# Window attention, forward and backward: GpSimd's gradient loads held until the gradient transpose ahead of them on SyncE has landed

## The chip, the cores and the metric

The kernel runs on one core of a Trainium2 chip. The metric is the device time of one execution in microseconds (us). A ratio is the mean time of one kernel's fast runs over the mean time of the other's fast runs of the same rounds on the same chip, with a 95% interval, so it is not quite the ratio of the medians that are quoted beside it. A run is called slow when it is over 1.5% above the fastest of the same kernel.

Words used throughout: a *transpose* is a DMA that SyncE issues and that turns a tile while it moves it; its *issue* is the time that SyncE spends on it, its *flight* the time from the start of the issue to landing. A *load* and a *store* are plain DMAs.

## The reference, cut to what matters

```python
xw  = windows of 8x8 tokens of x (1, 256, 256, 384)         # 1024 windows of 64 tokens
q, k, v = split(xw @ wqkv)
p   = softmax(q @ k.T * 384**-0.5)
out = windows_back((p @ v) @ wo)
out_0          = out
out_1, 2, 3    = gradients of x, wqkv, wo for a given grad_out
```

Everything is bf16. The kernel uses products of the weights that are formed once, so a window needs its x, its gradient and both of them transposed.

## The kernel before

The 1024 windows are handled eight at a time: 128 "quads" of four pairs. Three quads are in work at once: in step i, quad i-1 (c) is finished, quad i (b) gets its scores and softmax, quad i+1 (a) is projected, and inputs are loaded for a quad further on.

```python
    def load(st):                       # inputs of a quad
        xq = grp.tile(..., bufs=10);  dq = qp.tile(..., bufs=6)
        for t in range(QUAD):
            nc.sync.dma_start(out=xq[:, t, :], in_=windows(x, st, 2 * t))           # SyncE
            nc.gpsimd.dma_start(out=dq[:, t, :], in_=windows(grad_out, st, 2 * t))  # GpSimd

    def load_turn(st):                  # SyncE: dT <- dq, then xT <- xq (12 blocks of 128x128 each)
    ...
    def to_tokens(st):                  # SyncE: tok <- yz, 24 blocks
    def turn(st):                       # SyncE: PS <- ps, 4 blocks
    ...
    def attend(st, pair):
        ...                             # matmuls; ScalarE copies the results to o and d tiles
        for dst, sb, outer in stores:   # six stores a call, 96 or 48 KB each
            nc.gpsimd.dma_start(...)
    ...
    def step(c, b, a, ahead):
        B(scores);  B(soft, 0..4) between B(uv, ...)
        A(project, 0, ...)              # reads dT
        B(soft, 5);  B(turn)
        if ahead is not None:
            load(ahead)
        C_(attend, (0, 1))              # first group of six stores
        A(project, 1, ...)              # reads xT
        A(to_tokens)
        C_(attend, (2, 3))              # second group of six stores
```

In the traces SyncE and GpSimd work their instructions off in program order. Per step SyncE's order is dT, xT, PS, four loads of xq, tok; GpSimd's is four loads of dq, six stores, six stores.

Of the kernel before, what the change touches and what calls it, by code (L numbers as in the profile page):

```python
# [22 lines left out]
def kernel(  # L23
# [21 lines left out]
    nc = tc.nc  # L45
# [61 lines left out]
    def windows(ap, st, first, count=2):  # L107
        row, col = st["at"]
        return ap[0, row + WIN * first:row + WIN * (first + count), col:col + WIN, :]
# [1 line left out]
    LO, HI = slice(0, WT), slice(WT, P)  # L111
    OTHER = {0: HI, WT: LO}

    def load(st):
        st["xq"] = xq = grp.tile([P, QUAD, C], BF16, tag="xq", name="xq", bufs=2 * GQ + 4)
        st["dq"] = dq = qp.tile([P, QUAD, C], BF16, tag="dq", name="dq", bufs=6)
        for t in range(QUAD):
            nc.sync.dma_start(out=xq[:, t, :], in_=windows(x, st, 2 * t))
            nc.gpsimd.dma_start(out=dq[:, t, :], in_=windows(grad_out, st, 2 * t))  # L119
# [59 lines left out]
    def over_k(ap, n=P):  # L179
        return ap.unsqueeze(2).broadcast_to([n, QUAD, WT])  # L180

    def soft(st, step):
        sd = st["sd"]
        if step == 0:
# [122 lines left out]
    def filler(n):  # L307
        while n and fill:
            try:
                next(fill[0])  # L310
                n -= 1
            except StopIteration:
                fill.pop(0)

    def step(c, b, a, ahead):


        def on(st):
            return (lambda f, *r: f(st, *r)) if st is not None else (lambda f, *r: None)
        C_, B, A = on(c), on(b), on(a)  # L320
        B(scores)
        B(soft, 0)
        B(uv, 0, 0)
        B(uv, 0, 1)
        B(soft, 1)
        B(uv, 1, 0)
        B(uv, 1, 1)
        B(soft, 2)
        B(soft, 3)
        B(uv, 2, 0)  # L330
        B(uv, 2, 1)
        for t in range(QUAD):
            A(grad_turn, t)
        B(uv, 3, 0)
        B(uv, 3, 1)
        B(soft, 4)
        for mo in range(CK):
            A(project, 0, mo)
        B(soft, 5)
        B(turn)  # L340
        if ahead is not None:
            load(ahead)
        filler(1)
        C_(attend, (0, 1))
        split[0] = True
        for mo in range(CK):
            A(project, 1, mo)
        A(to_tokens)
        filler(1)
        split[0] = ALL  # L350
        C_(attend, (2, 3))
# [4 lines left out]
    sts = [{"at": q, "i": i} for i, q in enumerate(quads)]  # L356
    n = len(sts)
    AHEAD = 3
    with tc.manual_schedule(engines=MANUAL):
        for i in range(min(AHEAD, n)):  # L360
            load(sts[i])
            if i < AHEAD - 1:
                load_turn(sts[i])
        held = []
        get = lambda i: sts[i] if 0 <= i < n else None
        for i in range(-1, n + 1):
            if AHEAD - 1 <= i + AHEAD - 1 < n:
                load_turn(sts[i + AHEAD - 1])
            step(get(i - 1), get(i), get(i + 1), get(i + AHEAD) if i >= 0 else None)
            if i > 0:  # L370
                held.append(sts[i - 1])
                sts[i - 1] = None
            if held and (len(held) == GQ or i == n):
                fill.append(gf_group(held))
                held = []
        split[0] = False
        filler(1 << 30)
# [62 lines left out]
```

## Time and profile before

| | before |
|---|---|
| time, median of 3 runs | 1999.15 us (1994.77 to 2006.96) |
| span of the profiled execution | 1989.7 us |
| TensorE busy | 1961.3 us |
| an undisturbed step | 15.13 us, all matmuls |
| SyncE's queue, period from tok to tok, mean of quads 15 to 117 | 15.17 us |
| of it issuing / gaps | 14.28 / 0.89 us |

The list of DMA issues on the page of the kernel before (count, then the median flight in us):

```profile
dT<-dq SPq DMA_TRANSPOSE x128, 6.6
xT<-xq SPq DMA_TRANSPOSE x128, 6.8
```

The tile view of tok, before: the issue's duration in ns (least, median, longest), then the flight:

```profile
L167 SPq DMA_TRANSPOSE tok<-yz x128: 3903/4722/7185, 26.2 to 1944.2; - x128
...
DMA to landing us min/median/max: 5.8/8.4/12.3
```

tok is the largest of the four transposes, with a median flight of 8.4 us.

### The profile page before, as it was taken

The numbers are of one execution on the slowest core, as the hardware profiler recorded it, in microseconds if no ns is written. First come the engines' busy times: TensorE is split into PE (matmuls) and PEld (weight loads), VectorE is DVE, ScalarE is ACT, GpSimd is POOL, SyncE is SP. The second block draws the span as 40 slices with busy tenths as digits, with TensorE's granted clock in tenths as the row PEclk, the third lists the DMA queues.
The fourth block names the chain that finished last, engine by engine and source line by source line (L and its number), as shares of the span: only waits on it lengthen the run. The fifth ranks groups of instructions, "written<-read, shape, count | busy, mean of one in ns | idle before, by whom it ended". The sixth has DMA issues, their size and how long they took to land.

```text
span 1989.7 us, 52374 instructions
## 1 busy us (share of the span) xinstructions
PE 1961.3 (99%) x19418; PEld 1122.4 (56%) x19418; DVE 1258.1 (63%) x2851; ACT 1453.4 (73%) x3341; POOL 1122.6 (56%) x2054
## 2 busy tenths in 40 slices
PE   7899999999999999999999999999999999999998
PEld 4455555555555555555555555555555555555555
DVE  4666666666666666666666666566666666666665
ACT  5777777777777777777777777677777777777774
POOL 3555555565556555555655555555555556555543
PEclk9999999999999999999999999999999999999999
DMA  9999999999999999999999999999999999999993
GB/s 202 224 207 222 209 213 226 220 215 225 211 216 223 215 213 214 227 220 217 220 213 219 221 217 210 219 218 223 220 216 216 211 224 214 225 214 219 213 206 102
DMA packets 1042272, 425.62 MB, mean 214 GB/s; under 512 B 925792, under 2 KB 1016672, under 8 KB 1042016
## 3 DMA queue, kind: packets, MB, share of 16 engines
q1 hardware_dynamic: 943312, 270.60, 81.5%
q0 software_dynamic: 98304, 151.39, 31.3%
q8 instruction: 152, 2.49, 0.5%
q14 instruction: 104, 0.85, 0.1%
q10 hardware_dynamic: 400, 0.29, 0.0%
HBM read 101.84 MB, written 101.84 MB: 102 GB/s over the span
## 4 chain that ended last, share of the span: by engine, by line
PE 91%; DMA 7%; ACT 1%; DVE 1%; issue 0%; POOL 0%; SPq 0%; ACTq 0%; POOLq 0%
PE pj L147 33%; PE pj L145 12%; PE pg L147 12%; PE pg L145 12%; PE pd L258 6%; PE pu L253 5%; PE sd L147 5%; PE pw L253 4%; DMA dT<-dq 4%; DMA PS<-ps 2%; ACT uq L229 1%; ACT vq L229 0%; DMA dq<-in_grad_out_dram 0%; DMA xT<-xq 0%; PE pd L253 0%
## 5 line engine op out<-in xcount | busy, mean ns | idle before, releaser
L292 POOL DMA_DIRECT2D out_dram<-o x256 | 139.1, 543 | 693.8 <-ACT o L264 686.4
L304 DVE TENSOR_TENSOR GF_acc<-pg,GF_acc 128x384 f32<-128x384 f32 x258 | 143.8, 557 | 522.5 <-PE pg L145 372.3
L264 ACT CAST o<-po 128x384 bf16<-128x384 f32 x512 | 221.4, 487 | 248.1 <-issue 247.7
L147 PEld LDWEIGHTS <-xT 128*128 128x128 bf16 x3072 | 291.8, 98 | 182.2
L147 PE MATMUL pj<-B_sb,xT 128*128 128x384 bf16 x1536 | 333.4, 326 | 0.0
L147 PE MATMUL pj<-AT_sb,xT 128*128 128x384 bf16 x1536 | 333.3, 326 | 0.0
L119 POOL DMA_DIRECT2D dq<-in_grad_out_dram x512 | 274.2, 548 | 72.5 <-DMA out_dram<-o 39.1
L147 PE MATMUL pj<-dT,BT_sb 128*128 128x512 bf16 x1152 | 269.7, 379 | 5.5 <-DMA dT<-dq 5.3
L145 PE MATMUL pj<-xT,A_sb 128*64 128x512 bf16 x2304 | 271.9, 381 | 1.9 <-DMA xT<-xq 1.8
L229 ACT CAST uq<-pj 128x384 bf16<-128x384 f32 x512 | 247.3, 483 | 31.5 <-PE pj L147 28.4
L229 ACT CAST vq<-pj 128x384 bf16<-128x384 f32 x512 | 250.0, 488 | 2.7 <-ACT uq L229 0.3
L264 ACT CAST d<-pd 128x384 bf16<-128x384 f32 x512 | 227.6, 512 | 0.2 <-ACT o L264 0.2
L147 PEld LDWEIGHTS <-xq 128*128 128x128 bf16 x1572 | 153.7, 98 | 114.8 <-issue 0.3
L145 PEld LDWEIGHTS <-xq 128*64 128x64 bf16 x3000 | 167.9, 110 | 88.9
L207 ACT COPY ps<-Pb 64x256 bf16<-64x256 bf16 x256 | 103.2, 403 | 149.7 <-DVE Pb L204 148.2
L163 ACT CAST yz<-pj 128x512 bf16<-128x512 f32 x384 | 208.5, 659 | 3.6 <-PE pj L145 3.5
L161 ACT CAST yz<-pj 128x512 bf16<-128x512 f32 x384 | 206.4, 645 | 0.3 <-PE pj L147 0.2
L145 PEld LDWEIGHTS <-A_sb 128*64 128x64 bf16 x2304 | 132.4, 110 | 100.2 <-DMA xT<-xq 2.3
L147 PEld LDWEIGHTS <-BT_sb 128*128 128x128 bf16 x1152 | 111.4, 98 | 131.4 <-DMA dT<-dq 11.3
L147 PE MATMUL pg<-Uq,xq 128*128 128x384 bf16 x1032 | 181.6, 326 | 0.0
L253 PE MATMUL pu<-xq,PS 64*64 64x384 bf16 x1024 | 174.9, 335 | 6.4 <-DMA PS<-ps 5.9
L258 PE MATMUL pd<-tok,ps 128*64 128x384 bf16 x1024 | 177.7, 344 | 0.0
(68 smaller groups left out, 3366.6 us busy)
## 6 DMA issues: line engine op xcount, KB each, us to landing
xq<-in_x_dram SPq DMA_DIRECT2D x512, 96.0 KB, 4.1
dq<-in_grad_out_dram POOLq DMA_DIRECT2D x512, 96.0 KB, 4.0
out_dram<-o POOLq DMA_DIRECT2D x256, 96.0 KB, 4.3
out_dram<-o POOLq DMA_DIRECT2D x512, 48.0 KB, 4.4
out_dram<-d POOLq DMA_DIRECT2D x256, 96.0 KB, 4.4
out_dram<-d POOLq DMA_DIRECT2D x512, 48.0 KB, 4.4
dT<-dq SPq DMA_TRANSPOSE x128, 6.6
xT<-xq SPq DMA_TRANSPOSE x128, 6.8
```

The source lines that it names most:

```text
L119: nc.gpsimd.dma_start(out=dq[:, t, :], in_=windows(grad_out, st, 2 * t))
L145: nc.tensor.matmul(out[h], lhsT=lhsT[:, h], rhs=rhs, start=start, stop=stop)
L147: nc.tensor.matmul(out, lhsT=lhsT, rhs=rhs, start=start, stop=stop)
L161: ENG[EV["z"][mo]](out=yz[:, mo, :, 0:4:3, :], in_=pj[:])
L163: ENG[EV["y"][mo]](out=yz[:, mo, :, 1:3, :], in_=pj[:])
L207: nc.scalar.copy(out=ps[h, :, w, :], in_=Pb[h, :, :])
L229: cp(out=dst[:, t, :], in_=pj[:])
L253: nc.tensor.matmul(at[o, :], lhsT=turned(st, lhs, t, h), rhs=st[rhs][h, t, :], **{"start": True, "stop": True, **fl})
L258: nc.tensor.matmul(pd[outer if w == 0 else 1 - outer][o, :], lhsT=st["ps"][:, t, w, :], rhs=st["tok"][:, :, t, w, :], **flags)
L264: nc.scalar.copy(out=sb[:], in_=src[outer][:])
L292: nc.gpsimd.dma_start(out=windows(dst, st, 2 * t0 + 1), in_=sb[:])
L304: nc.vector.tensor_tensor(out=GF_acc[:, f, ma, :], in0=pw[:], in1=GF_acc[:, f, ma, :], op=ALU.add)
```

## The change

The gradient loads for a quad are to wait until the dT of the quad ahead has landed, so that they and the stores after them don't share the DMA engines with it. A copy of one element from that dT into the tile to be loaded makes GpSimd wait.

```diff
-    def load(st):
+    def load(st, behind=None):
         ...
+        if behind is not None:
+            nc.gpsimd.tensor_copy(out=dq[0:1, 0, 0:1], in_=behind[0:1, 0, 0, 0:1])
         for t in range(QUAD):
             nc.sync.dma_start(out=xq[:, t, :], in_=windows(x, st, 2 * t))
             nc.gpsimd.dma_start(out=dq[:, t, :], in_=windows(grad_out, st, 2 * t))
@@ step
         if ahead is not None:
-            load(ahead)
+            load(ahead, sts[ahead["i"] - 1]["dT"])
```

## The prediction

> **What bounds the kernel now.** I read the page first (busy time, DMA rows, issues), then the waits of TensorE's matmuls and weight loads, then the timelines of GpSimd and of SyncE's queue over two steps in the middle, and last the tile view of dT.
>
> ```profile
> PE 1961.3 (99%) x19418; PEld 1122.4 (56%) x19418; DVE 1258.1 (63%) x2851; ACT 1453.4 (73%) x3341; POOL 1122.6 (56%) x2054
> ...
> PEld L147 <- DMA dT<-dq: 11.3, 17, 1.5
> PEld L253 <- DMA PS<-ps: 9.0, 12, 3.5
> ...
> PE pu L253 <- DMA PS<-ps: 5.9, 5, 3.2
> PE pj L147 <- DMA dT<-dq: 5.3, 9, 1.1
> PE pj L145 <- DMA xT<-xq: 1.8, 1, 1.8
> ```
>
> TensorE is busy in 99% of the span. The wait rows (us in total, times, longest) say what all transposes together cost it in 128 steps: at the weight loads 11.3 us for dT and 9.0 us for PS. The last three rows are waits of the matmuls; those for PS and dT are the same waits seen a second time and are not added, the one for xT adds 1.8 us. The sum is 22.1 us, 1.1% of 1989.7 us. In the timeline the scores of successive steps begin at 1004.53 and 1019.66, so an undisturbed step takes 15.13 us, all of it back-to-back matmuls; the step from 1246.60 to 1263.0 took 16.4 us because its first matmuls on dT waited. So TensorE bounds nearly every step, and the transposes only a few of them. The chain of waits credits 4% of the span to dT<-dq, but that counts each transpose's whole flight of about 6.6 us, most of which lies beside matmuls.
>
> The second resource at its limit is the pair of SyncE's queue and the DMA engines:
>
> ```profile
> 999.70 2.84 SPq L128 DMA_TRANSPOSE dT<-dq  x1
> 1002.72 2.85 SPq L128 DMA_TRANSPOSE xT<-xq  x1
> 1005.73 1.20 SPq L233 DMA_TRANSPOSE PS<-ps  x1
> 1006.98 2.55 SPq L118 DMA_DIRECT2D xq<-in_x_dram  x4
> 1009.63 5.32 SPq L167 DMA_TRANSPOSE tok<-yz  x1
> 1015.18 1.45 SPq L128 DMA_TRANSPOSE dT<-dq  x1
> ```
>
> Columns are start, duration, engine, line, transfer. From one dT to the next are 15.48 us with gaps of 0.25 us at most: this queue works without a pause, at the pace of TensorE. Its margin is almost nil, which is why lateness of dT lasts for several steps once it appears.
>
> GpSimd's queue over the same time:
>
> ```profile
> 999.85 0.55 POOL L292 DMA_DIRECT2D out_dram<-o  x1 [4.62 <-ACT o L264]
> ...
> 1004.93 0.54 POOL L292 DMA_DIRECT2D out_dram<-o  x1 [1.75 <-ACT o L264]
> ...
> 1008.21 2.14 POOL L119 DMA_DIRECT2D dq<-in_grad_out_dram  x4
> 1014.98 0.55 POOL L292 DMA_DIRECT2D out_dram<-o  x1 [4.62 <-ACT o L264]
> ...
> DMA to landing us min/median/max: 3.9/6.6/9.6
> ```
>
> Six stores at 999.85, right on top of the dT issued at 999.70; six more at 1004.93; the four gradient loads at 1008.21. The last line is the flight of dT. 12 stores and 4 loads of about 0.55 us are 8.8 us of issue in 15.13, so GpSimd has about 6 us to spare.
>
> **What the Trainium skill says.** "DMA: Bandwidth & Descriptors", section "Issuing engines are not separate DMA queues": transfers issued from any engine run on the same 16 DMA engines and interleave. The trace agrees: the same 12-block transpose flies between 3.9 and 9.6 us, though its size never changes. The same page, "Anatomy of one DMA", says that DMA engines do not wait on semaphores; the wait is on the issuing sequencer before dispatch. That matters here: GpSimd's one-element copy holds everything after it in GpSimd's order, stores included. "GPSIMD Engine Reference", section "2.1 Instruction dispatch", warns that consecutive Pool instructions are not a barrier: a later Pool instruction needs the completion semaphore of the earlier one; the built program has exactly such a wait of the first load on the copy.
>
> **The change part by part.**
> Added: one copy of one element on GpSimd for each of 125 held loads. No row of this trace has such a copy; I estimate 0.4 us with its wait and completion, 50 us of GpSimd over the span, all inside its spare 6 us a step. The order of the built instructions shows nothing else added or removed on any engine; 512 loads, 768 stores and 512 transposes stay.
>
> Moved: which dT the copy waits for. The loads at 1008.21 belong to the quad after the one whose dT is issued next, at 1015.18. That dT lands at about 1015.2 + 6.6 = 1021.8. So this is no small nudge: the loads move from 1008.2 to about 1022, by 13.6 us, almost a step. The stores of the following step, ready from 1014.98 on, move behind them: in place of two groups of six at 1015.0 and 1020.1 there is one burst of twelve from about 1024.4 to 1031 or later.
>
> What this gives: the time from about 8 us before a dT to its landing has fewer of GpSimd's packets. dT now shares its flight with six stores; afterwards with the tail of a burst at most. I expect its flight to fall from 6.6 to about 5 or 5.5 us (the minimum is 3.9). xT gains likewise. tok, which overlaps the burst, loses; but tok causes no wait in this trace and is wanted only half a step or more after it lands. Total bytes and packets are unchanged, so the work of the DMA engines is unchanged, and SyncE's queue should keep a period near 15.1 us. Of the 22.1 us of waits the dT share of 11.3 us could go mostly; I credit 5 us, because PS and the lag of the queue itself remain.
>
> What this costs: the slack of the gradient loads. Before, loads issued at 1008.2 landed near 1008.2 + 1.65 + 4.0 = 1013.9 (three further issues of 0.55 us, then the page's median flight of 4.0 us), and their dT came one step later, at about 1030.2: 16 us of slack. Afterwards there is a closed loop: dT lands (6.6), copy (0.4), issues (1.65), last load lands (4.0), next dT. Sum 12.7 us, against a step of 15.13: it closes with 2.4 us to spare. It overruns only where dT and load are both slow (9.6 and a load near 8 or 10 us). I take 10% of the steps overrunning by 1 us, much of it absorbed since dT is issued some 3 us before it is needed: 12 us lost at most, 4 us credited.
>
> Stores: the o and d staging tiles have 8 buffers each, two steps' worth. A delay of about 9 us leaves more than half a step. I count zero.
>
> Sum: -5 + 4 = about -1 us, with fewer dT waits by shorter flight and a few by late loads. Against the median of 1999.15 us that is 1998; I lean slightly to the good side, 1996.
>
> **The rivals.**
> (1) The loop becomes the bound. If the flights in the new arrangement sum to 15.5 us, each step takes 15.5 and the kernel loses 128 x 0.4 = 50 us: about 2045. For it: the median margin is 2.4 us and the maxima exceed it, and SyncE's queue, once held by a late load, also delays xT, PS, xq and tok behind it. Against it: the loads now enter a GpSimd queue that has been empty for microseconds, in place of following six stores, so they should land faster than 4.0 us from issue.
> (2) A real gain. If SyncE's queue gets shorter without the stores under dT and xT, all 22 us of waits could go: about 1977. No more than that is to be had, because the rest of the span is matmuls; a gain over 2% (40 us) would need the matmuls themselves to shorten. This is why I hold it nearly impossible.
> (3) A store burst that stalls ScalarE: output tiles not free in time. It would show as waits of o and d copies on out_dram. Against it: two steps of buffers; it could cost some 20 us if landing took a whole step.
>
> **Range and chances.** From the best case (1977) and a modestly overrunning loop (0.2 us a step, 25 us, about 2022), and from runs of the unchanged kernel that lie between 1994.77 and 2006.96: 1980 to 2022. Faster by over 2%: 2%. Slower by over 2%: 8%, rival 1. Within 2%: 90%.
>
> **What would show it.** Loads of GpSimd begin within 1 us after a dT landing, with the wait of the copy of some 5 us a step; stores come in one burst of twelve; dT's median flight is below 6.6 us, tok's above 8.4; total TensorE waits on transposes stay between 5 and 30 us; undisturbed steps remain 15.13 us. The prediction is wrong if SyncE's queue shows dT waiting for dq in a large share of the steps, or steps of more than 15.3 us on the average.

## More of the kernel before

The experiments were made in six groups; the kernel before was run beside each, and its median there lay between 1993.78 and 2005.56 us.

A transfer is *outstanding* from the start of its issue to its landing.

## The result, and the profile after

| | before | after |
|---|---|---|
| time, median of 4 runs each | 1996.96 us (1990.1 to 2006.96) | 2112.98 us (2107.65 to 2114.43) |
| ratio, 95% interval | 1 | 1.0572 (1.0522 to 1.0622) |
| span, profiled execution | 1989.7 us | 2111.0 us |
| TensorE's idle time (span less busy time) | 28.4 us | 122.1 us |

The changed kernel is slower by 5.7%. Its busy line and its waits for transposes (total us, times, longest):

```profile
PE 1988.9 (94%) x19418; PEld 1119.6 (53%) x19418; DVE 1258.5 (60%) x2851; ACT 1459.8 (69%) x3341; POOL 1143.6 (54%) x2179
```

```profile
PEld L149 <- DMA dT<-dq: 143.2, 100, 4.5
...
PE pj L149 <- DMA dT<-dq: 98.1, 78, 4.1
...
PEld L255 <- DMA PS<-ps: 1.9, 5, 0.8
```

Weight loads now wait for dT in 100 of 128 steps, for 143.2 us in place of 11.3. In the median dT landed 2.2 us before its first matmul began in the kernel before, and 0.05 us before it now. These waits are not all lost, since a weight load starts while the matmul before it runs; the matmuls' own 98.1 us is nearer to the loss. The whole loss of 121.3 us of span is 93.7 us more idle time of TensorE (122.1 - 28.4) and 27.6 us more busy time (1988.9 - 1961.3). Only dT does this: the waits for PS shrank from 9.0 to 1.9 us.

Yet dT itself flies no longer than before. The page's list of issues, after:

```profile
dq<-in_grad_out_dram POOLq DMA_DIRECT2D x512, 96.0 KB, 3.2
...
dT<-dq SPq DMA_TRANSPOSE x128, 6.6
xT<-xq SPq DMA_TRANSPOSE x128, 5.8
```

So dT is not slow; it is issued late. SyncE's timeline over two steps says why (start, duration, line, transfer):

```profile
1025.63 2.50 SPq L130 DMA_TRANSPOSE dT<-dq  x1
1028.30 3.07 SPq L130 DMA_TRANSPOSE xT<-xq  x1
1031.53 1.19 SPq L235 DMA_TRANSPOSE PS<-ps  x1
1032.78 2.51 SPq L120 DMA_DIRECT2D xq<-in_x_dram  x4
1035.39 6.86 SPq L169 DMA_TRANSPOSE tok<-yz  x1
1042.49 1.68 SPq L130 DMA_TRANSPOSE dT<-dq  x1
```

From dT to dT are 16.86 us here. Nothing stands between the entries: SyncE waits for no data here. (The view of SyncE's waits books 582.3 us in front of tok to ScalarE's yz. That is no such wait: tok's issue begins 10.9 us in the median, and never less than 8.2 us, after the last part of yz is written, against 8.2 and 6.3 us in the kernel before.) The entry that grew is tok, 6.86 us against 5.32 in the step that the prediction shows. The tile view of tok, after, confirms it for the whole run:

```profile
L169 SPq DMA_TRANSPOSE tok<-yz x128: 3957/6050/7858, 22.5 to 2065.5; - x128
...
DMA to landing us min/median/max: 5.8/11.3/13.5
```

What goes on beside tok is in GpSimd's timeline over the same step (in brackets the idle time before and what ended it):

```profile
1032.22 0.18 POOL L118 COPY dq<-dT 1x1 bf16<-1x1 bf16 x1 [6.19 <-DMA dT<-dq]
1032.79 2.14 POOL L121 DMA_DIRECT2D dq<-in_grad_out_dram  x4 [0.39 <-POOL dq L118]
1034.88 0.57 POOL L294 DMA_DIRECT2D out_dram<-o  x1
...
1038.20 0.54 POOL L294 DMA_DIRECT2D out_dram<-o  x1
...
1044.90 0.56 POOL L292 DMA_DIRECT2D out_dram<-d  x1
```

The copy waits 6.19 us for dT, as intended; the loads go out at 1032.79; and then the stores that had to stand behind them go out, from 1034.88, in a run. That is exactly where tok (1035.39 to 1042.25) is being issued. I counted, from issue and landing of every store, how many were outstanding on the average while tok was issued: 0.8 before, 5.3 after.

SyncE's queue by kind of issue, worked out from the start and end of every DMA issue of SyncE in the trace (means, quads 15 to 117, us a step, the period from tok to tok):

| | dT | xT | PS | 4 xq | tok | issues | gaps and waits | period |
|---|---|---|---|---|---|---|---|---|
| before | 2.14 | 3.01 | 1.49 | 2.74 | 4.89 | 14.28 | 0.89 | 15.17 |
| after | 2.35 | 2.97 | 1.34 | 2.47 | 6.03 | 15.16 | 1.04 | 16.20 |
| difference | +0.21 | -0.04 | -0.15 | -0.27 | +1.14 | +0.88 | +0.15 | +1.03 |

1.03 us times 128 steps is 132 us, beside 121 us of lost span. The 0.15 us is SyncE's wait for late gradient loads (21.1 us in nine waits in the whole run). The loss is thus a longer period of SyncE's queue, and of that 1.14 us is tok, 0.15 late loads, and the rest nearly cancels.

A smaller part has to do with TensorE's clock. The timeline of TensorE and the view by stretches (us, busy time of PE, PEld, DVE, ACT, POOL with counts, granted clock, DMA share, GB/s), after:

```profile
1015.05 3.53 PE L149 MATMUL pj<-dT,BT_sb 128*128 128x512 bf16 x9 [2.36 <-DMA dT<-dq]
```

```profile
1015.00:1019.00 4.00, 3.95 (x11) 1.52 (x12) 0.50 (x2) 1.88 (x4) 3.58 (x7) 0.57 1.00 227
```

After an idle gap of 2.36 us the granted clock was 0.57 over the next 4 us, and the nine matmuls on dT took 3.53 us; at full clock a step later they took 2.12 us. There were seven such stretches inside the loop, one before. They account for some 12 of the 27.6 us of longer busy time (lost clock summed over the records: 14.7 us after, 3.1 before).

### The profile page after: what moved, and what is told of

Read it like the earlier page. It is cut to its first block, busy times and chain, and to the rows that moved or that the text cites. A ratio compares the mean times of both kernels' runs of the same rounds, so it can differ in the third digit from the quotient of the medians.

```text
span 2111.0 us, 52749 instructions
## 1 busy us (share of the span) xinstructions
PE 1988.9 (94%) x19418; PEld 1119.6 (53%) x19418; DVE 1258.5 (60%) x2851; ACT 1459.8 (69%) x3341; POOL 1143.6 (54%) x2179
## 2 busy tenths in 40 slices
DMA packets 1042274, 425.64 MB, mean 202 GB/s; under 512 B 925792, under 2 KB 1016672, under 8 KB 1042016
## 5 line engine op out<-in xcount | busy, mean ns | idle before, releaser
L149 PE MATMUL pj<-dT,BT_sb 128*128 128x512 bf16 x1152 | 280.1, 390 | 105.6 <-DMA dT<-dq 98.1
L149 PEld LDWEIGHTS <-BT_sb 128*128 128x128 bf16 x1152 | 106.6, 99 | 257.7 <-DMA dT<-dq 143.2
L118 POOL COPY dq<-dT 1x1 bf16<-1x1 bf16 x125 | 26.2, 210 | 394.9 <-DMA dT<-dq 357.0
L294 POOL DMA_DIRECT2D out_dram<-d x256 | 138.6, 542 | 181.8 <-DMA out_dram<-o 66.0
L291 POOL DMA_DIRECT2D out_dram<-d x256 | 144.1, 563 | 126.5 <-ACT d L266 52.7
L292 POOL DMA_DIRECT2D out_dram<-d x256 | 144.1, 563 | 82.2 <-DMA out_dram<-d 68.7
```

What stands on the lines that cost most here:

```text
L149: nc.tensor.matmul(out, lhsT=lhsT, rhs=rhs, start=start, stop=stop)
L291: nc.gpsimd.dma_start(out=windows(dst, st, 2 * t1 + 1, 1), in_=sb[LO, :])
L292: nc.gpsimd.dma_start(out=windows(dst, st, 2 * t0, 1), in_=sb[HI, :])
L294: nc.gpsimd.dma_start(out=windows(dst, st, 2 * t0 + 1), in_=sb[:])
```

## The experiments

Two theories at the start. **Queue**: the held stores come out in a burst while SyncE issues tok; tok's issue gets longer, SyncE's in-order queue falls behind TensorE, and dT is late. **Loop**: dT, copy, loads, next dT form a closed circle that has become the bound. Below, "stores at tok" is the average number of outstanding stores during tok's issue; period, issues and tok are means worked out as above. dT wait is that of the weight loads.

| run | median us | ratio (95%) | period | issues | gaps, waits | tok issue | stores at tok | dT wait |
|---|---|---|---|---|---|---|---|---|
| before | 1996.96 | 1 | 15.17 | 14.28 | 0.89 | 4.89 | 0.8 | 11.3 |
| after | 2112.98 | 1.057 (1.052-1.062) | 16.20 | 15.16 | 1.04 | 6.03 | 5.3 | 143.2 |
| d_older | 1992.16 | 0.999 (0.994-1.004) | 15.17 | 14.27 | 0.90 | 4.80 | 0.7 | 14.6 |
| b_last | 2024.47 | 1.015 (1.011-1.020) | 15.46 | 13.88 | 1.58 | 4.63 | 0.7 | 33.0 |
| c_stores | 2083.57 | 1.044 (1.040-1.048) | 16.01 | 15.10 | 0.90 | 5.72 | 6.0 | 100.6 |
| a_between | 2105.14 | 1.054 (1.048-1.060) | 16.20 | 15.12 | 1.08 | 5.97 | 5.2 | 139.9 |
| e_tok | 2114.74 | 1.058 (1.056-1.060) | 16.15 | 15.25 | 0.90 | 5.72 | 4.6 | 151.7 |
| h_pause | 2001.82 | 1.004 (0.999-1.010) | 15.36 | 14.46 | 0.90 | 4.44 | 1.4 | 44.1 |
| i_later | 2054.73 | 1.030 (1.027-1.033) | 15.76 | 14.86 | 0.89 | 5.12 | 1.2 | 74.2 |
| l_tiny | 2004.32 | 1.005 (1.003-1.007) | 15.25 | 14.35 | 0.90 | 4.62 | 0.6 | 10.8 |
| s_swap | 2041.05 | 1.018 (1.014-1.022) | 15.63 | 14.72 | 0.90 | 5.18 | 4.2 | 43.2 |
| v_burst | 2091.87 | 1.047 (1.043-1.051) | 16.01 | 15.12 | 0.89 | 5.47 | 3.6 | 122.1 |
| w_xq | 2039.35 | 1.022 (1.019-1.025) | 15.62 | 14.27 | 1.35 | 4.51 | 0.4 | 28.3 |
| t_drop (wrong result) | 1977.02 | 0.987 (0.983-0.990) | 15.03 | 12.06 | 2.97 | 4.24 | 2.1 | 1.4 |
| u_drop (wrong result) | 1979.72 | 0.992 (0.990-0.994) | 15.09 | 13.87 | 1.22 | 4.74 | 1.0 | 0 |
| x_after_act | 2021.26 | 1.013 (1.010-1.015) | 15.46 | 11.81 | 3.65 | 4.96 | 2.3 (estimate) | 3.1 |
| y_before_act (3 fast runs) | 2075.13 | 1.040 (1.037-1.044) | 15.88 | 14.30 | 1.58 | 5.85 | 6.3 | 30.4 |
| z_half_act | 1988.36 | 0.996 (0.994-0.999) | 15.14 | 13.79 | 1.35 | 5.21 | 5.2 | 1.1 |

One thing to see before the single runs: in before, c_stores, d_older, e_tok, h_pause, i_later, l_tiny, s_swap and v_burst the gaps are 0.89 or 0.90 us. There SyncE waits for nothing between its issues, and its period is the sum of its issues plus this constant. It's these issues that stretch and shrink. This sum says where the time is, not what made it; for that the runs have to be compared. f_after_xq and g_before_xq, two failed tests, are left out of the table. In x_after_act the trace lacks the landing of 644 of the 1536 stores; they are counted with the median flight of their kind. The profiled execution of h_pause was the slowest of its four, 2016 us, so the last five entries of its row are on the bad side.

### What the copy costs

d_older keeps all 125 copies, but each asks for a dT one quad older, which has long landed.

```diff
-            load(ahead, sts[ahead["i"] - 1]["dT"])
+            load(ahead, sts[ahead["i"] - 2]["dT"])
```

> The copy reads the dT of one quad earlier, which has landed by then: same 125 copies, nothing is held. Both theories: 1990 to 2010. If the copies themselves cost (a third theory, C), above 2030.

1992.16 us, the same as before (the interval is -0.6 to +0.4%). The copies as such are free; all that follows comes from when transfers start.

### Loads late, stores free

b_last puts the copy and the four gradient loads at the end of GpSimd's step, behind both groups of stores, so no store stands behind the copy's wait but those of the next step.

```diff
         C_(attend, (2, 3))
+        if ahead is not None:
+            load_grad(ahead, sts[ahead["i"] - 1]["dT"])   # copy and four dq loads; xq loads stay
```

> The copy and loads stand behind both store groups, so no store is held; the loads are issued at the same place within the step as before the change, for a quad that is one step nearer. Theory A: 1990 to 2015, tok issue near 4.8. Theory B (loads too close to their own dT): slower than 2090, with SyncE's queue waiting for dq in most steps.

1.5% slower, not 5.7%, between the ranges of the two theories. SyncE's issues are even shorter than before (13.88 us), tok's is 4.63 us; the loss comes from SyncE waiting for gradient data, 94.9 us in 44 waits against 21.1 in nine in the changed kernel. Late loads cost something when they come this late, but it is another cost than the one sought.

### Stores late, loads free

c_stores issues the loads unheld and puts the same wait, with a copy into a spare tile, between them and the first group of stores.

```diff
-            load(ahead, sts[ahead["i"] - 1]["dT"])
+            load(ahead)
+            hold = sm.tile([P, 1], BF16, tag="hold", name="hold")
+            nc.gpsimd.tensor_copy(out=hold[0:1, 0:1], in_=sts[ahead["i"] - 1]["dT"][0:1, 0, 0, 0:1])
```

> The copy stands behind the loads and writes a scratch tile: loads are never short of slack, but all twelve stores of a step wait for the dT and go out in one burst. Theory A: as slow as the changed kernel, 2080 to 2130, tok issue about 6. Theory B: 1990 to 2010.

4.4% slower: most of the loss with loads that are in good time (SyncE waited for them 6.3 us in three waits). The circle through the loads is not needed for it. Six stores are outstanding during tok's issue, and that issue is 5.72 us. This points to Queue.

### Only one group of stores held

I took the harm for that of a run of twelve, made because the first group has to wait. a_between therefore puts the copy and loads between the two groups.

```diff
         C_(attend, (0, 1))
+        if ahead is not None:
+            load_grad(ahead, sts[ahead["i"] - 1]["dT"])
         split[0] = True
```

> The copy and the four gradient loads stand between the two store groups of a step; the loads still wait for the same dT and start at the same time as in the changed kernel, only the first six stores go out undelayed. Theory A (the loss comes from the twelve delayed stores that go out in one burst under the tok transpose and stretch its issue on SyncE's queue, 6.05 us against 4.7): most of it comes back, time below 2040, tok issue median below 5.3. Theory B (the closed loop dT, copy, loads, dT sets the period of 16.2): loop unchanged, time 2095 to 2125.

5.4% slower: a miss for me, with a time in the range that Loop (B in the expectation) gave. GpSimd's timeline in this run shows that I had rearranged nothing:

```profile
1000.19 2.13 POOL L127 DMA_DIRECT2D dq<-in_grad_out_dram  x4 [0.39 <-POOL dq L125]
1002.29 0.56 POOL L300 DMA_DIRECT2D out_dram<-o  x1
...
1005.62 0.54 POOL L300 DMA_DIRECT2D out_dram<-o  x1
```

The second group stands behind the loads, and the first group of the next step right behind the second: again loads and a long run of stores, at the same place on the clock. An order that repeats every step has no beginning; only the place of the wait in the circle counts.

### The burst moved away from tok, by tok's own landing

e_tok holds the stores of the kernel before until that step's tok has landed.

```diff
             load(ahead)
+        if b is not None and c is not None:
+            hold = sm.tile([P, 1], BF16, tag="hold", name="hold")
+            nc.gpsimd.tensor_copy(out=hold[0:1, 0:1], in_=b["tok"][0:1, 0, 0, 0, 0:1])
```

> As c_stores, but the copy waits for the landing of the tok transpose and not of a dT: again all twelve stores of a step are held and go out in one burst, only now after tok. Theory A' (what costs is stores lying under the tok transpose, wherever they were ready): tok issue below 4.9 us, period back at 15.13, time 1985 to 2015. Theory D (any hold of stores or any burst of twelve costs, by delay or by crowding): 2050 to 2130, as c_stores.

5.8% slower, another miss. tok lands so late that twelve stores after it are still being worked off when the next tok is issued: 4.6 stores at tok, tok's issue 5.72 us. The stores missed one tok's flight and met the next one's issue. The run doesn't speak against Queue, but the edit didn't do what I meant.

### The loads of x moved to GpSimd: two failed tests

To give SyncE slack I let GpSimd issue the four loads of x, in the changed kernel (f_after_xq) and in the kernel before (g_before_xq).

```diff
-            nc.sync.dma_start(out=xq[:, t, :], in_=windows(x, st, 2 * t))
+            nc.gpsimd.dma_start(out=xq[:, t, :], in_=windows(x, st, 2 * t))
```

> The changed kernel with its four xq loads a step issued by GpSimd ahead of the copy, so that SyncE's queue has 2.6 us less to issue a step. Theory A (SyncE's queue, stretched by tok to 16.2 us a step, is the new bound): its period falls under 15.13 and the time comes back to 1985 to 2030. Theory B or any theory in which the chain through dT and the loads is the bound: 2090 or more.

> The kernel before with the same move of the xq loads; control for f_after_xq and a candidate that beats it. Theory A: SyncE's queue gets slack, the waits on transposes (22 us) shrink: 1975 to 1995. If GpSimd with 20 transfers a step is too full: above 2000.

2305.87 us (1.154, 1.148 to 1.160) and 2271.1 us (1.136, 1.133 to 1.139). With 20 transfers a step GpSimd delivers gradients too late: SyncE waited for them 547.3 and 422.8 us in total. The tests replaced one overload by another and tell nothing of the change. They do tell something of tok: its issue took 6.22 and 6.46 us with only 1.9 and 2.1 stores beside it, so stores are not all that counts. The right engine for this test was ScalarE; see the last group.

### The pause at other places

h_pause lets the loads wait for the softmax of the same step (the tile ps), about the moment at which GpSimd stood idle anyway; i_later leaves the loads free and holds the first group of stores until the last projection of the step is written.

```diff
-            nc.gpsimd.tensor_copy(out=dq[0:1, 0, 0:1], in_=behind[0:1, 0, 0, 0:1])
+            nc.gpsimd.tensor_copy(out=dq[0:1, 0, 0:1], in_=behind[0:1, 0, 1, 0:1])
@@ step
-            load(ahead, sts[ahead["i"] - 1]["dT"])
+            load(ahead, b["ps"])
```

> No store is held and no load waits for a dT: the loads wait for the step's own ps, a TensorE-paced event, and so move from about S+3.7 to S+7.8 (S: start of the scores), into GpSimd's pause; they keep some 12 us of slack. Theory A'' (what counts is that GpSimd has nothing outstanding while tok, 24 of the 52 transposed blocks of a step, is in flight; the pause of the kernel before lies just there): tok stretches to 5.3 or more, GpSimd transfers outstanding under tok rise from 4.0 to above 5, time 2040 to 2110. Theory D (holds, bursts or the loop through dT cost): none is left here, 1990 to 2010.

```diff
         A(to_tokens)
+        if c is not None:
+            if a is not None:
+                nc.gpsimd.tensor_copy(out=hold[0:1, 0:1], in_=a["yz"][0:1, CK - 1, 0, 1, 0:1])
+            put(c)                      # the six stores that attend (0, 1) had issued itself
```

> The kernel before with the first store group of each step held until the y projection is copied (S+12.8, 2.5 us later than now), which makes the pause under tok longer. Theory A'': tok and dT land earlier, the waits on transposes shrink: 1975 to 1992. Theory D: a hold costs here too, above 2010. If the pause is long enough already: 1990 to 2005.

h_pause: 0.4% slower with an interval that includes none. The form of Queue tested here (A'': anything of GpSimd's outstanding at tok costs) missed, with tok at 4.44 us where 5.3 or more was expected, but the edit did not crowd tok: with the loads counted too, 4.9 transfers are outstanding at its issue, as before. A wait of GpSimd is harmless if it lies where GpSimd pauses anyway. i_later: 3.0% slower, where A'' expected a gain, although only 1.2 stores are outstanding at tok. The means of its issues say where the time is: the issues of dT, xT, PS and tok grew by 0.20, 0.18, 0.11 and 0.23 us and xq's shrank by 0.12, in sum 0.58. No single transfer is to blame there. The burst at tok does not explain this run.

### How much slack SyncE has

l_tiny is the kernel before with one small load added to SyncE's queue behind every tok.

```diff
         A(to_tokens)
+        if a is not None:
+            tiny = sm.tile([P, 8], BF16, tag="tiny", name="tiny")
+            nc.sync.dma_start(out=tiny[:], in_=x[0, 0, 0:P, 0:8])
```

> The kernel before with one further small load a step (128 rows of 16 bytes) issued by SyncE, about 0.6 us of its queue and hardly any bytes. If SyncE's queue has no slack, as theory A says, each step grows by up to 0.5 us: 2030 to 2075. If the queue only looks full because it waits inside its instructions: 1990 to 2010.

The extra issue took 0.59 us a step, and the period grew by 0.08 only: the other issues became shorter by 0.52 us in sum, xT by 0.33 and tok by 0.27. An issue is thus no fixed cost. At 2004.32 us the run missed what Queue expected (2030 to 2075) and fell into the range of the other case, that the queue only looks full because it waits inside its instructions. So SyncE being occupied all the time does not mean that each added issue costs its own length. That it is the DMA engines that an issue waits for is my reading and not shown.

### Loads and second stores exchanged

s_swap makes the second group of stores wait for the next step's softmax, behind the gradient loads.

```diff
+            nc.gpsimd.tensor_copy(out=dq[0:1, 0, 0:1], in_=behind[0:1, 0:1])        # behind: last d tile
             ...                                                                     # four dq loads
+            nc.gpsimd.tensor_copy(out=hold[0:1, 0:1], in_=b["ps"][0:1, 0, 1, 0:1])
+            put(*late.pop())                                                        # second group
         C_(attend, (0, 1))                                                          # first group
```

> Everything TensorE-paced, nothing waits for a dT: loads go out at about S+1 to S+3 (after the last d copy), the second store group of a step waits until the next step's ps is written and goes out at S+7.8 to S+11, the first group follows at once. So stores, not loads, fill GpSimd's pause; h_pause put loads there and lost 0.4%. Theory S (stores outstanding while xq and tok are issued stretch tok, and through it SyncE's queue): stores outstanding during tok's issue above 3, tok issue above 5.4 us, time 2050 to 2110. Theory L (only waits tied to a transpose's landing cost, by locking GpSimd and SyncE to each other): 1990 to 2015.

1.8% slower, between the ranges of the two theories and half-way in every column: 4.2 stores at tok, tok's issue 5.18 us, period 15.63 us.

### Fewer stores

t_drop leaves out the stores of out_1 in the changed kernel, u_drop in the kernel before. Their outputs are wrong, which doesn't matter for the times.

```diff
+        held = len(stores)
         keep("d", out_1, pd)
+        del stores[held:]
```

> The changed kernel without the six stores of out_1 a step (a wrong result on purpose): holds, copies and the loop through dT and the loads unchanged, half of the store bytes gone. Theory S: the burst ends earlier, tok issue falls under 5.2 us, the period back to 15.13 to 15.3, time 1985 to 2030. Theory B or L (a chain of waits sets the period): 2080 or more.

> Control for t_drop: the kernel before without the stores of out_1 (wrong on purpose). It shows the floor of the matmuls with transposes that are never late: all theories 1965 to 1985, with the hold of t_drop (1977) costing less than 10 us.

1977.02 and 1979.72 us. With the held loads in full force, TensorE is busy all the time in t_drop. The view by stretches over a thousand us of it, and its waits for dT:

```profile
900.00:1900.00 1000.00, 1000.00 (x9986) 574.39 (x9984) 640.38 (x1452) 746.71 (x1719) 379.81 (x727) 1.00 0.97 193
```

```profile
PEld L149 <- DMA dT<-dq: 1.4, 4, 0.7
```

This is the hardest blow to Loop: the circle dT, copy, loads, dT is there unaltered and costs nothing. SyncE's issues sum up to 12.06 us, and tok's begins 0.02 us (median) after its source is written, where it began 10.9 us after in the changed kernel. The queue no longer lags. The two runs also show the floor set by the matmuls, about 1977 to 1980 us. The kernel before is thus within 1% of it.

### The same burst without a tie to a transpose, and a tie without a burst at tok

v_burst issues the loads unheld and lets all twelve stores wait for the row maximum of the next step's scores, a moment set by TensorE. w_xq is c_stores with another wait: the stores wait for the last load of x on SyncE.

```diff
# v_burst, in attend, then behind the second uv of the next step
+        late.append((st, stores, t0, t1))           # in place of issuing
+                nc.gpsimd.tensor_copy(out=hold[0:1, 0:1], in_=b["mx"][0:1, 0:1])
+            while late:
+                put(*late.pop(0))
```

> The kernel before with all twelve stores of a step held until the next step's mx is written (TensorE-paced, about S+2.2): the same burst of twelve as in c_stores, at about the same place in the step, loads behind it, but not tied to the landing of any transpose. Theory S (place of the stores: under xq and tok): tok issue above 5.4, 2050 to 2100, like c_stores (2084). Theory L (the tie of the burst to SyncE's own queue is what costs beyond s_swap's 1.8%): 2010 to 2045.

```diff
# w_xq
             load(ahead)
+            nc.gpsimd.tensor_copy(out=hold[0:1, 0:1], in_=ahead["xq"][0:1, QUAD - 1, 0:1])
```

> As c_stores, but the burst of twelve waits for the landing of the xq loads, so it is tied to SyncE's queue and goes out when tok's issue is nearly over, under tok's tail and the next dT. Theory S: stores outstanding during tok's issue below 2.5, tok issue below 5.2, time 1995 to 2050. Theory L: 2070 to 2130.

v_burst is 4.7% slower. Its GpSimd and its SyncE:

```profile
1009.14 0.17 POOL L333 COPY hold<-mx 1x1 f32<-1x1 f32 x1 [5.79 <-DVE mx L187]
...
1016.32 2.15 POOL L119 DMA_DIRECT2D dq<-in_grad_out_dram  x4
```

```profile
1013.53 6.17 SPq L167 DMA_TRANSPOSE tok<-yz  x1
```

Twelve stores between 1009.7 and 1016.3, and a tok of 6.17 us that begins in the middle of them. No GpSimd instruction waits for a transpose here, so the delay needs no circle. w_xq has a burst as long, tied to SyncE, but most of it falls between tok's issues:

```profile
1005.88 0.18 POOL L344 COPY hold<-xq 1x1 bf16<-1x1 bf16 x1 [5.10 <-DMA xq<-in_x_dram]
```

```profile
1002.85 4.22 SPq L167 DMA_TRANSPOSE tok<-yz  x1
...
1017.87 4.82 SPq L167 DMA_TRANSPOSE tok<-yz  x1
```

tok keeps its short issue (4.51 us in the mean) and SyncE's issues their old sum (14.27 us). The 2.2% that this kernel loses come from elsewhere: its gradient loads stand behind the twelve stores, and SyncE waits for gradients 57.4 us in 24 waits. That is the 0.45 us by which its gaps exceed 0.90.

### Slack for SyncE with a right result

The last group lets ScalarE issue the loads of x: all four in the changed kernel (x_after_act), all four in the kernel before (y_before_act), two of four in the kernel before (z_half_act). All results are correct.

```diff
-            nc.sync.dma_start(out=xq[:, t, :], in_=windows(x, st, 2 * t))
+            nc.scalar.dma_start(out=xq[:, t, :], in_=windows(x, st, 2 * t))
# z_half_act: (nc.scalar if t >= 2 else nc.sync).dma_start(...)
```

> The changed kernel with the four loads of x issued by ScalarE in place of SyncE. Same transfers, same held gradient loads, same burst of stores. Queue theory: over the middle of every run so far SyncE's period is the sum of its issue times plus about 0.9 us of gaps plus its waits for gradient data (before 14.28 + 0.89, changed 15.16 + 0.9 + 0.15). Without the loads of x the sum of the changed kernel is about 15.2 - 2.5 = 12.7 us, so the queue can run in about 13.6 us and has 1.5 us to spare in a step of TensorE; the burst may still lengthen the issue of the token transpose, but nobody waits for it. Expected: time 1980 to 2010 us, weight-load waits for dT under 20 us, the token transpose starting within 1 us of its source in most steps. Rival L (the loop dT, copy, loads, dT or dT's own flight is the limit): time stays near 2110. Rival E: ScalarE, at 11.1 us of work a step plus 2.5 us of issue, becomes the bound: idle TensorE with waits on ScalarE, 2020 to 2100, and few waits for dT.

> The kernel before with the four loads of x issued by ScalarE. Queue theory: SyncE's sum falls to about 11.6 us, the 22 us of transposes' waits vanish: 1975 to 1985 us unless ScalarE's added 2.5 us of issue a step holds TensorE (rival E: 2020 us or more). Beside x_after_act it tells whether held loads cost anything once the queue has slack: queue theory within 0.5% of each other, rival L over 3% apart.

> The kernel before with two of the four loads of x issued by ScalarE: half the relief for SyncE (sum about 13 us, a spare of 1.2 us), half the burden for ScalarE (12.4 us of 15.1). Queue theory: 1976 to 1986 us, about 0.7% better than before, with correct results; if ScalarE holds TensorE already with half, above 1996.

In x_after_act the waits for dT are gone; the first line is TensorE's, the second that of SyncE's queue:

```profile
PEld L149 <- DMA dT<-dq: 3.1, 3, 2.3
```

```profile
SPq L130 <- DMA dq<-in_grad_out_dram: 373.7, 190, 7.5
```

SyncE now really waits for the held loads, 373.7 us of it, and still dT comes in time: the circle closes within a step once the queue has slack. So far as Queue said, though tok still begins 4.0 us (median) after its source, where less than 1 us was expected. The time, 2021.26 us, is above the 1980 to 2010 that I expected: TensorE has few waits left but is busy 1986.8 us for the same matmuls, 25.5 us more than before. The traces say where. First the kernel before, then x_after_act:

```profile
1013.98 0.56 DVE L277 CAST Wq<-pw 128x384 bf16<-128x384 f32 x1 [0.19 <-PE pw L253]
...
1014.37 1.03 PE L145 MATMUL pj<-xT,A_sb 128*64 128x512 bf16 x8
```

```profile
1014.95 0.56 DVE L279 CAST Wq<-pw 128x384 bf16<-128x384 f32 x1 [0.19 <-PE pw L255]
...
1015.56 0.81 PE L147 MATMUL pj<-xT,A_sb 128*64 128x512 bf16 x5
```

In the kernel before, the first matmul on xT begins while VectorE's copy of Wq is still running, 0.17 us before its end. In x_after_act it begins 0.05 us after the end, in each of 103 steps that I read, and its record names a wait for VectorE's semaphore that the record in the kernel before does not have. The distance from the matmul ahead of it adds up to 50.6 us over the run, against 25.8 before. An undisturbed step thus takes 15.37 us and not 15.13, in y_before_act too, but not in z_half_act. It has nothing to do with late transfers, nor is it the ScalarE bound (2020 to 2100 us) that the expectation named as a rival: the largest row of TensorE's waits for ScalarE is 5.4 us. Why the built program has this wait is open.

y_before_act was a plain miss, 2075.13 us where I expected 1975 to 1985. Without any copy 6.3 stores are outstanding at tok, whose issue takes 5.85 us, xT's 4.13 in place of 3.01. But SyncE had slack: it paused before tok in 38 of 102 steps, by 0.9 us a step in the mean beyond the usual gap. Some 31 us of the loss are the longer undisturbed step (128 times 0.24); the rest, some 50 us of 81 us of span, is in steps in which TensorE waited for transposes in spite of the slack (its weight loads 30.4 us for dT and 27.7 us for PS). So slack in SyncE's mean period is not enough. With the loads of x on ScalarE the change is a gain, by 54 us: the changed kernel has the better meeting of transfers there.

z_half_act has stores at tok (5.2) and a tok of 5.21 us, but two issues fewer on SyncE; the sum is 13.79 us, tok begins 0.38 us (median) after its source, and TensorE waits 1.1 us for dT. At 1988.36 us, just above the range that I expected, it's the one version with right results that beats the kernel before, by 0.4% (interval 0.1 to 0.6%).

### What is settled and what is open

Settled: the changed kernel loses its time because SyncE's queue takes 1.03 us longer a step and so comes too late to dT; tok's issue alone is 1.14 us longer, and the other changes nearly cancel. The burst at tok does it with no circle through a transpose (v_burst), the same burst at another place leaves tok short (w_xq), and the circle alone costs nothing (t_drop). Runs with over 3 stores outstanding at tok have a tok of 5.2 to 6.0 us (after, a_between, c_stores, e_tok, s_swap, v_burst, y_before_act, z_half_act), those with 2.3 or fewer one of 4.2 to 5.1, except f_after_xq and g_before_xq. These two fit as well if all plain transfers are counted, loads of gradients and of x besides the stores: 4.9 are outstanding at tok before, 7.7 after, 7.0 in either of the two; all ten runs with 6.4 or more have a tok of 5.2 to 6.5 us, all ten with 5.7 or fewer one of 4.2 to 5.1. So it may be the number of transfers beside tok that counts, and not that they are stores. (A slow transfer is outstanding for longer, so the count is in part an effect.) The longer tok costs time where SyncE has no slack (after, a_between, c_stores, e_tok, s_swap and v_burst, with gaps of 0.9 to 1.1 us) and none in z_half_act, which has some; y_before_act has slack and loses all the same.

Open: what an issue waits for. The rival that no run excludes is that the 16 DMA engines together are near their limit and SyncE's issues only show it: the DMA row of the page is at 9 tenths in nearly all slices before and after. The bytes alone are not that limit, since x_after_act, with the same transfers and the same holds, moved 211 GB/s against 202 in the changed kernel. Open too: why i_later stretches all four transposes a little; what disturbs y_before_act; why TensorE waits for VectorE in the programs with all loads of x on ScalarE.

## Why the prediction was wrong

**The step that failed** is "Total bytes and packets are unchanged, so the work of the DMA engines is unchanged, and SyncE's queue should keep a period near 15.1 us". The bytes are indeed unchanged (425.62 and 425.64 MB). The period became 16.20 us. An issue of SyncE is no constant of a transfer: tok's went from 4.89 to 6.03 us because of what ran beside it.

**The step beside it** is "tok, which overlaps the burst, loses; but tok causes no wait in this trace". It foresaw that tok's flight would grow (8.4 to 11.3 us) and took a transfer that nobody waits for as harmless. (Nobody does: tok still lands 5.6 us, in the median, before its first matmul; 9.3 before.) What counts is not tok's landing but that SyncE can't go on to dT while it issues tok. The prediction had itself said of this queue that it works without a pause and that its margin is almost nil; it did not draw the consequence.

**dT's flight** was to fall from 6.6 to 5 or 5.5 us. It stayed 6.6: the tail of the burst lies under it, 7.6 outstanding stores during its issue against 3.4 before (the same count as for tok; the prediction had said six). xT's did fall, from 6.8 to 5.8, and the waits for PS from 9.0 to 1.9 us.

**Stores: "I count zero".** Right for the reason given, that output tiles suffice, and wrong as a sum, since the delayed stores are what lengthened tok.

**What held.** The move of the loads until after dT, though it was larger: they went out 3.7 us (median) after the start of the step's scores before and 22.2 us now, 18.5 us later and not 13.6, most of the difference because dT itself lands 4 us later against TensorE's step. Also the single run of stores, the copy at no cost (d_older), and the sum of the loop: the last gradient load landed 3.4 us (median) before SyncE issued the dT that needs it, so the circle has slack. The loads' flight shortened from 4.0 to 3.2 us. The undisturbed step of 15.13 us is still there. One count in the prediction is wrong, without weight in its sum: there are 1536 stores, 768 for each of two outputs.

**The rivals.** The first had the sign, steps over 15.3 us, and the wrong cause: it made the loop the bound, which t_drop, c_stores and x_after_act refute. The second's floor of 1977 us is just what t_drop reached. The third, waits for output tiles, wasn't seen. What was missing is a fourth: a transfer that nobody waits for can lengthen its own issue, in an in-order queue that works without a pause. The view that would have priced it is the tile view of tok in the kernel before: its issue lasts between 3903 and 7185 ns for one and the same size, 4722 in the median, so this entry alone could take 2.5 us of a step (7185 - 4722) from a queue that works without a pause. That the bunched transfers would lengthen it had to be tried.

## What to carry to other kernels

When transfers are moved, ask of every in-order queue that issues DMAs whether it is occupied all the time; if it is, a longer issue there can delay whatever stands behind it, whoever waits for its own data, as tok's did here (4.89 to 6.03 us) with more transfers beside it. But being occupied is not proof of having no slack: l_tiny added 0.59 us of issue a step and lost 0.08. A wait placed in a queue delays all that stands behind it, and in a loop that is the next step's work too: draw the whole circle and see what the delayed part will meet. Slack for the queue is worth a trial, but no rule: two loads moved to another engine won 0.4% here, all four lost 4.0%.

## What the Trainium skill lacked or had wrong

- "DMA: Bandwidth & Descriptors", section "Issuing engines are not separate DMA queues", says that the time to initiate a DMA is "usually small relative to the DMA itself". For the transposes of SyncE it is not: tok's issue took 4.72 of 8.4 us of flight before and 6.05 of 11.3 after (medians).
- The same page, section "Rules for kernel authors", says that a transpose next to ordinary DMAs needs nothing. That is meant for correctness, and all results here agree with it (but for the two runs that drop stores on purpose); no page names the price. Here tok's issue became 1.14 us longer with 5.3 in place of 0.8 stores outstanding beside it, and the kernel 5.7% slower.
- No page has it, for transfers within a core, that an issue stretches and gives way: 0.59 us of added issue a step (l_tiny) lengthened the queue's period by 0.08 us only, while dropping six of GpSimd's sixteen transfers a step (t_drop) shortened SyncE's issues from 15.16 to 12.06 us in sum.
- "TensorE: Matmul & The Clock Gate", section "HAM oscillation — how this bites in real kernels", gives as the rule no idle gaps above some 3.4 us. Here the clock fell to 0.57 over the 4 us that followed a gap of 2.36 us, in one of seven such stretches; five of the seven followed gaps of 2.1 to 3.2 us, while gaps of 2.22 and 2.35 us elsewhere left it at full.
